# One visit of two token tiles moved from the late to the early list of a mixture layer

## The chip, the cores and the metric

The kernel runs on one core of a Trainium2 chip. The metric is the device time of one execution in microseconds. The engines are TensorE (PE), which multiplies matrices; VectorE (DVE), ScalarE (ACT) and GpSimd (POOL), which work element by element; and SyncE (SP), which issues the DMAs here. Each engine takes its instructions strictly in the order of its own program and waits on semaphores of the others.

## What is computed

Three layers in a row, all float32: attention in which each query keeps its 32 best keys; a soft mixture of 8 experts whose shares are normalised 8 times over rows and columns; and a mixture in which each token goes to its one best expert, with 288 places for each.

```python
def _moe_ref(x, w_gate, w1, w2):
    logits = x @ w_gate                       # x: 1152 x 512, 8 experts
    logits = logits - logits.max()
    P = np.exp(logits)
    for _ in range(8):
        P /= P.sum(1, keepdims=True) + 1e-09
        P /= P.sum(0, keepdims=True) + 1e-09
        P *= N / E
    for e in range(E):
        h = np.maximum(x @ w1[e], 0.0)        # 512 -> 1024
        ye = h @ w2[e]                        # 1024 -> 512
        out += P[:, e:e + 1] * ye
    return out.astype(np.float32)
```

The change concerns this middle layer. Attention before it gives x, and the third layer takes out.

## The kernel before

The 1152 tokens lie in 9 tiles of 128. A **visit** (e, a, b) computes expert e for tiles a to b-1: it goes through the 1024 hidden values in 8 blocks, and each block needs one pair of weight tiles, 128 x 512 each, of w1 (`w0h`, `w0l` in the rows, first matmuls on line 1041) and of w2 (`w1h`, `w1l`, second matmuls on line 1153). The products are float32 by parts: each operand is cut into a high part in a reduced format (`h`) and the rest (`l`), and three of the four part products are added up. A visit of two tiles has, for each block, 12 first matmuls of 256 columns and 6 second matmuls of 512, 144 in all.

Cutting a weight tile takes a load into a raw buffer (`ra`, `rb`; SyncE), a copy to the high part (ScalarE, line 975) and a subtraction for the rest. The subtraction is here called a **split**. In an early visit it is on GpSimd (line 981), in a late one on VectorE (line 978). The first matmul's result goes through ScalarE (`hh`, line 989) and VectorE (`hl`, line 991).

Early visits run beside the attention, before the shares P are known. Their sums are parked: ScalarE copies one out of PSUM (line 1142), SyncE stores it in DRAM, and later loads it again (line 1188) for VectorE to add it, times the share, to `acc` (line 1178). Late visits run when the attention is done; their sums go from PSUM to `acc` directly. Both kinds hold their first matmuls' left operands in three or four buffers, so weights can be prepared two to three blocks ahead.

Between the two lists stands the **normalisation** (`sinkhorn`, lines 1192 to 1232): 8 passes in a strict chain. In a pass VectorE runs four small instructions over rows (lines 1212 to 1215: reduce, add a constant, reciprocal, multiply), TensorE one matmul with a matrix of ones (line 1225, two records), and VectorE four over columns (lines 1218 to 1221, the same kinds).

The order of every engine's program is fixed when the kernel is built. A planner (`Order`) simulates all engines with a cost for each job and puts the jobs down as they would start; jobs with a lower rank go first among those that are ready. Visits have ranks that rise in the order of the two lists; the normalisation has the lowest, so it goes ahead of everything that is ready. The planner's costs know nothing of what engines do to each other. After the late visits of tiles 2 to 5, tiles 6 to 8 are visited, and the tokens of finished tiles are routed in between (from line 1688 on: transposes, line 1721, line 1766), and GpSimd sends their rows out with indirect DMAs (line 1781).

Of the kernel before, what the change touches and what calls it, by code (L numbers as in the profile page):

```python
# [23 lines left out]
PARTIAL = 2  # L24
WITH = 3
FILL = 390.0
EARLY = [(0, 0, 1), (1, 0, 1)] + [(e, 0, 2) for e in range(2, 8)] + [(0, 1, 4), (1, 1, 4), (2, 2, 4), (3, 2, 6), (4, 2, 6), (0, 4, 6), (1, 4, 6)]
LATE = [(5, 2, 6), (6, 2, 6), (7, 2, 6), (2, 4, 6)] + [(e, 6, 9) for e in (2, 3, 4, 5, 6, 7, 0, 1)]
ALONE = 16
FIRST = 16  # L30
ROWS = 16
# [188 lines left out]
class Net:  # L220
# [777 lines left out]
    def mixture_one(self):  # L998
        self.unit, self.chain = 0, {}
        self.left = {t: [] for t in range(self.NT)}  # L1000
        self.visits_first(PARTIAL)
        for n, v in enumerate(EARLY):
            if n < PARTIAL:
# [6 lines left out]
    def late_one(self):  # L1010
        for v in LATE[:-1]:
            self.visit(*v, whole=v[2] - v[1] == 3)
        self.visit(*LATE[-1], whole=True)
        seen = sorted((e, t) for e, a, b in EARLY + LATE for t in range(a, b))
        assert seen == [(e, t) for e in range(self.E) for t in range(self.NT)]
# [218 lines left out]
    def made_late(self, mem):  # L1234

        def more(pool, other):
            pool.free += [(self.o.t["X"], t) for _, t in other.free]
        n = LATE[-1]
        self.ff = mem.tile([128, 16, (n[2] - n[1]) * 128], F32R, name="f")
# [590 lines left out]
```

## Time and profile before

| what | before |
|---|---|
| median of 3 runs | 1176.47 us (1176.34 to 1177.87) |
| the profiled execution | 1177.07 us |
| its span, first to last instruction | 1175.2 us |
| granted TensorE clock, mean | 0.998 of full speed |
| TensorE busy | 1151.5 us (98%) |
| VectorE busy | 907.2 us (77%) |
| ScalarE busy | 729.5 us (62%) |
| GpSimd busy | 440.5 us (37%) |

A busy share over the whole span hides the stages. Up to about 565 us TensorE and VectorE are both busy nearly all the time (attention and early visits); then comes the normalisation; from 600 us on the late visits and the routing; from 1040 us the third layer. The views used are the busy time by windows, the list of waits, and the timelines of single engines, which give each instruction with its start, its length and the idle time before it.

### The profile page before, as it was taken

The page shows a single profiled execution, that of the slowest core. Times are in us where ns is not written, and L with a number is a line of the kernel's source. Part 1 is how long each engine was busy: PE and PEld are TensorE (multiplying, and loading weights), DVE is VectorE, ACT ScalarE, POOL GpSimd, SP SyncE. Part 2 cuts the span into 40 slices and gives each one's busy share as a digit, 9 for nine tenths or more (in the row PEclk, how much of TensorE's full clock was granted, in tenths as well). Part 3 has the DMA queues.
Part 4 walks back from the last instruction along what each step waited for, and adds up shares of the span by engine and source line. Part 5 has one row for each costly group of instructions (what it writes and reads, how often), then busy time and mean ns, then how long its engine had stood idle before and what let it go on. Part 6 is the DMA issues. An engine that isn't in the chain of part 4 may idle for free.

```text
span 1175.2 us, 20867 instructions
## 1 busy us (share of the span) xinstructions
PE 1151.5 (98%) x6607; PEld 1005.3 (86%) x6607; DVE 907.2 (77%) x2178; ACT 729.5 (62%) x1731; POOL 440.5 (37%) x403
## 2 busy tenths in 40 slices
PE   8999999999999999999999999999999999999997
PEld 5877888888889888888888888989999999898886
DVE  7998999999999999998655567844555555568882
ACT  7666889888788877768543334543334444258882
POOL 5466877777556744547500000100000000016541
PEclk9999999999999999999999999999999999999999
DMA  5467666655444655536555555643444444279980
GB/s 141 110 173 204 200 182 186 190 167 156 138 134 111 201 164 148 164 109 187 153 184 175 161 171 155 204 135 114 130 125 144 144 131 136 75 238 358 344 273 23
DMA packets 243607, 195.08 MB, mean 166 GB/s; under 512 B 67551, under 2 KB 186335, under 8 KB 243488
## 3 DMA queue, kind: packets, MB, share of 16 engines
q1 hardware_dynamic: 241232, 188.78, 53.8%
q0 software_dynamic: 1648, 4.73, 1.0%
q8 instruction: 54, 0.88, 0.3%
q14 instruction: 65, 0.53, 0.2%
q10 hardware_dynamic: 608, 0.15, 0.1%
HBM read 172.87 MB, written 21.33 MB: 165 GB/s over the span
## 4 chain that ended last, share of the span: by engine, by line
PE 54%; DVE 31%; ACT 6%; issue 5%; DMA 2%; POOL 1%; SPq 0%; POOLq 0%; DVEq 0%; ACTq 0%
PE yp L1041 14%; PE yp L1153 12%; PE tp L1153 8%; DVE wk L773 7%; PE tp L1041 6%; DVE m L775 6%; DVE e L784 3%; DVE hl L991 2%; DVE m L769 2%; PE yp L1372 2%; DVE wk L719 2%; DVE etl L830 2%; DVE m L721 1%; PE tp L264 1%; PE tp L1388 1%
## 5 line engine op out<-in xcount | busy, mean ns | idle before, releaser
L1781 POOL DMA_INDIRECT disp<-acc,idx x9 | 10.3, 1141 | 436.7 <-DVE run L1777 436.7
L981 POOL TENSOR_TENSOR w0l<-ra,w0h 128x512 fp32r<-128x512 f32 x104 | 134.8, 1296 | 95.0 <-ACT w0h L975 88.3
L981 POOL TENSOR_TENSOR w1l<-rb,w1h 128x512 fp32r<-128x512 f32 x104 | 134.7, 1296 | 49.8 <-ACT w1h L975 45.6
L975 ACT ACTIVATE w0h<-ra 128x512 fp32r<-128x512 f32 x211 | 131.9, 626 | 0.0
L775 DVE MAX8 m<-wk 128x8 f32<-128x576 f32 x168 | 125.0, 751 | 1.1
L975 ACT ACTIVATE w1h<-rb 128x512 fp32r<-128x512 f32 x148 | 93.3, 630 | 52.3 <-PE yp L1153 41.3
L1041 PE MATMUL yp<-xh,w0h 128*128 128x256 f32 (+2 forms) x528 | 107.2, 325 | 0.3 <-DVE hl L991 0.2
L1041 PE MATMUL yp<-xl,w0h 128*128 128x256 f32 (+2 forms) x528 | 106.7, 324 | 0.0
L1041 PE MATMUL yp<-xh,w0l 128*128 128x256 f32 (+2 forms) x528 | 106.6, 323 | 0.0
L1153 PE MATMUL yp<-w1h,hh 128*128 128x512 f32 x240 | 98.0, 408 | 0.4 <-DVE hl L991 0.4
L989 ACT ACTIVATE hh<-yp 128x256 fp32r<-128x256 f32 (+3 forms) x113 | 49.6, 439 | 76.3 <-PE yp L1041 60.0
L1041 PEld LDWEIGHTS yp<-xh,w0h 128*128 128x128 f32 x528 | 87.7, 188 | 10.1 <-DVE hl L991 1.6
L1153 PE MATMUL yp<-w1l,hh 128*128 128x512 f32 x240 | 94.2, 393 | 0.0
L1153 PE MATMUL yp<-w1h,hl 128*128 128x512 f32 x240 | 94.1, 392 | 0.0
L975 ACT ACTIVATE v<-rb 128x512 fp32r<-128x512 f32 x65 | 40.5, 629 | 79.5 <-PE yp L1153 41.8
L991 DVE SCALAR_TENSOR_TENSOR hl<-yp,hh 128x256 fp32r<-128x256 f32 (+3 forms) x113 | 55.2, 488 | 44.2 <-ACT hh L989 43.7
L1041 PEld LDWEIGHTS yp<-xh,w0l 128*128 128x128 f32 x528 | 85.1, 189 | 3.8
L1041 PEld LDWEIGHTS yp<-xl,w0h 128*128 128x128 f32 x528 | 85.0, 189 | 3.9
L1153 PE MATMUL yp<-v,f 128*128 128x512 f32 x360 | 84.4, 391 | 0.0
L773 DVE MATCH_REPLACE8 wk<-m,wk 128x576 f32<-128x576 f32 x112 | 83.2, 743 | 0.4
L1153 PEld LDWEIGHTS yp<-v,f 128*128 128x128 f32 x360 | 67.2, 188 | 13.5
L978 DVE TENSOR_TENSOR w0l<-ra,w0h 128x512 fp32r<-128x512 f32 x107 | 73.5, 687 | 0.4
(555 smaller groups left out, 3026.2 us busy)
## 6 DMA issues: line engine op xcount, KB each, us to landing
rb<-in_moe_w_dram SPq DMA_DIRECT2D x248, 256.0 KB, 3.0
ra<-in_moe_w_dram SPq DMA_DIRECT2D x245, 256.0 KB, 3.1
acc<-in_moe_w_dram SPq DMA_DIRECT2D x67, 256.0 KB, 6.0
y<-ys SPq DMA_DIRECT2D x33, 256.0 KB, 2.4
ys<-y SPq DMA_DIRECT2D x23, 256.0 KB, 3.0
vr<-in_v_dram SPq DMA_DIRECT2D x40, 128.0 KB, 2.8
disp<-z SPq DMA_DIRECT2D x6, 771.0 KB, 5.0
qg<-in_q_dram SPq DMA_DIRECT2D x63, 64.0 KB, 2.6
```

What stands on the lines that cost most here:

```text
L719: j = self.job("DVE", r, 0.73, lambda i=i: nc.vector.match_replace(wk.t, m.t[:, i], flat() if i == 0 else wk.t, LOW), deps=[j], take=[wk] ...
L769: j = j0 = self.job("DVE", r, 0.66, lambda: nc.vector.max(m.t[:, 0], flat()), deps=got, take=[m])
L773: j = self.job("DVE", r, 0.73, lambda i=i: nc.vector.match_replace(wk.t, m.t[:, i], flat() if i == 0 else wk.t, LOW), deps=[j], take=[wk] ...
L775: j = self.job("DVE", r, 0.66, lambda i=i: nc.vector.max(m.t[:, i + 1], wk.t), deps=[j], use=[wk] if i == 2 else [])
L784: masks.append(self.job("DVE", r, t_dve(288) + 0.08, lambda half=half, p=p: nc.vector.scalar_tensor_tensor(e.t[:, half * 288:(half + 1) * ...
L975: jh = self.job("ACT", -500 + rank, t_act(512, True), lambda r=r, w=w: nc.scalar.activation(w.t[0], r.t, AF.Copy), deps=[j], take=[w])
L978: jl = self.job("DVE", -100 + rank, t_dve(512, True), lambda r=r, w=w: nc.vector.tensor_sub(w.t[1], r.t, w.t[0].bitcast(F32)), deps=[jh], ...
L981: jl = self.job("POOL", -100 + rank if k > 8 * NATIVE + 4 else FIRST - 3, t_pool(512), lambda r=r, w=w: nc.gpsimd.tensor_sub(w.t[1], r.t, ...
L989: jh = self.job("ACT", -1000 + k * 0.001, t_act(b - a), lambda: nc.scalar.activation(h.t[0][:, a:b], p.t[:, :b - a], AF.Relu), deps=deps, ...
L991: jl = self.job("DVE", -1000 + k * 0.001, t_dve(b - a), lambda: nc.vector.scalar_tensor_tensor(h.t[1][:, a:b], p.t[:, :b - a], 0.0, h.t[0] ...
L1041: nc.tensor.matmul(p.t[:, :b - a], w1[0].t[i][:, d, :], self.xt[s][:, d, c0 + a:c0 + b], start=m == 0 and d == 0, stop=m == 2 and d == 3)
L1153: nc.tensor.matmul(y[t].t, h.t[i][:, c:c + 128], w2[0].t[s], start=f == 0 and m == 0, stop=f == last and m == 2)
```

## The change

The visit of expert 2, tiles 4 and 5, leaves the late list and becomes the last entry of the early list.

```diff
-EARLY = [(0, 0, 1), (1, 0, 1)] + [(e, 0, 2) for e in range(2, 8)] + [(0, 1, 4), (1, 1, 4), (2, 2, 4), (3, 2, 6), (4, 2, 6), (0, 4, 6), (1, 4, 6)]
-LATE = [(5, 2, 6), (6, 2, 6), (7, 2, 6), (2, 4, 6)] + [(e, 6, 9) for e in (2, 3, 4, 5, 6, 7, 0, 1)]
+EARLY = [(0, 0, 1), (1, 0, 1)] + [(e, 0, 2) for e in range(2, 8)] + [(0, 1, 4), (1, 1, 4), (2, 2, 4), (3, 2, 6), (4, 2, 6), (0, 4, 6), (1, 4, 6), (2, 4, 6)]
+LATE = [(5, 2, 6), (6, 2, 6), (7, 2, 6)] + [(e, 6, 9) for e in (2, 3, 4, 5, 6, 7, 0, 1)]
```

With that its 16 splits go to GpSimd, its two sums are parked and fetched back, and it stands ahead of the visit of expert 5. No instruction of TensorE is added or dropped. The two lists already end and begin in the middle of the normalisation, so the visit lands there.

GpSimd's program around the end of the early visits, before (`w0l`, `w1l` are the rests of the weight tiles; the last row is the first indirect DMA of the routing):

```order
L981 TENSOR_TENSOR w0l_80<-ra_75,w0h_79 128x512
L981 TENSOR_TENSOR w1l_90<-rb_77,w1h_89 128x512
L981 TENSOR_TENSOR w0l_82<-ra_73,w0h_81 128x512
L981 TENSOR_TENSOR w1l_92<-rb_76,w1h_91 128x512
L1781 DMA disp<-acc,idx_6557 2304x514
```

and after, from the same place on:

```order
L981 TENSOR_TENSOR w0l_82<-ra_73,w0h_81 128x512
L981 TENSOR_TENSOR w1l_92<-rb_76,w1h_91 128x512
L981 TENSOR_TENSOR w0l_84<-ra_74,w0h_83 128x512
L981 TENSOR_TENSOR w1l_86<-rb_78,w1h_85 128x512
L981 TENSOR_TENSOR w0l_80<-ra_75,w0h_79 128x512
L981 TENSOR_TENSOR w1l_88<-rb_77,w1h_87 128x512
L981 TENSOR_TENSOR w0l_82<-ra_73,w0h_81 128x512
```

Behind `w1l_92`, where the indirect DMAs of the routing followed, there are now sixteen more splits, of which five are shown.

VectorE's program at the fourth pass of the normalisation, before and after in one piece of the difference:

```order
 L1215 TENSOR_TENSOR prob<-prob,rsum 128x72
 L991 SCALAR_TENSOR_TENSOR hl_98<-yp_72,hh_97 128x256
-L978 TENSOR_TENSOR w0l_84<-ra_74,w0h_83 128x512
-L978 TENSOR_TENSOR w1l_86<-rb_78,w1h_85 128x512
 L1218 TENSOR_REDUCE csum<-tp_65 128x8
 L1219 TENSOR_SCALAR csum<-csum 128x8
 L1220 RECIPROCAL csum<-csum 128x8
 L1221 TENSOR_TENSOR prob<-prob,csum 128x72
-L991 SCALAR_TENSOR_TENSOR hl_94<-yp_71,hh_93 128x256
 L1212 TENSOR_REDUCE rsum<-prob 128x9
 L1213 TENSOR_SCALAR rsum<-rsum 128x9
```

The splits of expert 5 have left the passes; the same holds for the passes behind.

TensorE's program at the fifth and sixth pass:

```order
 L1153 MATMUL tp_67<-w1h_87,hl_98 128x512
 L1041 MATMUL tp_66<-xh,w0h_81 128x256 x4
+L1225 MATMUL tp_68<-prob,ones 128x72
 L1041 MATMUL tp_66<-xl,w0h_81 128x256 x4
 L1041 MATMUL tp_66<-xh,w0l_82 128x256 x4
-L1225 MATMUL tp_68<-prob,ones 128x72
 L1153 MATMUL yp_69<-w1h_89,hh_93 128x512
 L1153 MATMUL yp_69<-w1l_90,hh_93 128x512
```

The fifth pass's matmul stands eight matmuls earlier, and from here on there is one pass's matmul in every block of the visit, in the same place.

## Rows read from the trace of the kernel before

**Rows 1.** Windows: us, busy us (count) of PE, PEld, DVE, ACT, POOL; clock; DMA.

```profile
582.00:600.00 18.00, 17.71 (x94) 15.03 (x93) 15.76 (x55) 7.99 (x16) 0.00 (x0) 1.00 0.56 175
...
600.00:1040.00 440.00, 439.53 (x2289) 391.60 (x2288) 251.70 (x539) 176.23 (x340) 10.27 (x9) 1.00 0.47 145
```

**Rows 2.** All waits of TensorE, 560 to 1050 us: total us, times, longest.

```profile
PE tp L1225 <- DVE prob L1215: 2.2, 2, 1.9
PE yp L1202 <- DVE sk L1201: 0.5, 1, 0.5
PE tp L1398 <- DVE hl L991: 0.5, 1, 0.5
```

**Rows 3.** TensorE timeline: start us, us, instruction, [idle before <- releaser].

```profile
571.60 0.34 PE L1225 MATMUL tp<-prob,ones 128*128 128x72 f32 x2
...
576.67 0.44 PE L1225 MATMUL tp<-prob,ones 128*128 128x72 f32 x2 [1.87 <-DVE prob L1215]
...
579.81 0.34 PE L1225 MATMUL yp<-prob,ones 128*128 128x72 f32 x2
...
583.30 0.44 PE L1225 MATMUL tp<-prob,ones 128*128 128x72 f32 x2 [0.29 <-DVE prob L1215]
```

**Rows 4.** GpSimd timeline, the weight splits around the same passes.

```profile
572.23 1.28 POOL L981 TENSOR_TENSOR w1l<-rb,w1h 128x512 fp32r<-128x512 f32 x1
...
574.02 1.28 POOL L981 TENSOR_TENSOR w0l<-ra,w0h 128x512 fp32r<-128x512 f32 x1 [0.51 <-ACT w0h L975]
...
575.26 1.27 POOL L981 TENSOR_TENSOR w1l<-rb,w1h 128x512 fp32r<-128x512 f32 x1
...
579.19 1.29 POOL L981 TENSOR_TENSOR w0l<-ra,w0h 128x512 fp32r<-128x512 f32 x1 [2.66 <-ACT w0h L975]
...
580.44 1.29 POOL L981 TENSOR_TENSOR w1l<-rb,w1h 128x512 fp32r<-128x512 f32 x1
```

**Rows 5.** VectorE timeline, small instructions of the normalisation.

```profile
569.31 0.15 DVE L1207 TENSOR_SCALAR sk<-sk 128x1 f32<-128x1 f32 x1
...
572.25 1.30 DVE L1219 TENSOR_SCALAR csum<-csum 128x8 f32<-128x8 f32 x1
...
574.35 0.98 DVE L1213 TENSOR_SCALAR rsum<-rsum 128x9 f32<-128x9 f32 x1
...
575.62 1.00 DVE L1215 TENSOR_TENSOR prob<-prob,rsum 128x72 f32<-128x72 f32 x1
...
578.85 0.23 DVE L1215 TENSOR_TENSOR prob<-prob,rsum 128x72 f32<-128x72 f32 x1
...
580.45 1.30 DVE L1219 TENSOR_SCALAR csum<-csum 128x8 f32<-128x8 f32 x1
...
582.02 0.23 DVE L1221 TENSOR_TENSOR prob<-prob,csum 128x72 f32<-128x72 f32 x1
...
582.55 0.17 DVE L1213 TENSOR_SCALAR rsum<-rsum 128x9 f32<-128x9 f32 x1
...
583.01 0.23 DVE L1215 TENSOR_TENSOR prob<-prob,rsum 128x72 f32<-128x72 f32 x1
```

**Rows 6.** ScalarE timeline: weight copies, and one copy of a finished sum.

```profile
578.49 0.62 ACT L975 ACTIVATE w0h<-ra 128x512 fp32r<-128x512 f32 x1
...
581.47 0.62 ACT L975 ACTIVATE w0h<-ra 128x512 fp32r<-128x512 f32 x1
...
582.58 0.63 ACT L975 ACTIVATE w1h<-rb 128x512 fp32r<-128x512 f32 x1 [0.48 <-PE tp L1153]
...
593.19 0.59 ACT L1142 ACTIVATE yt<-yp 128x512 f32<-128x512 f32 x1
```

**Rows 7.** VectorE groups, 560 to 600 us: busy us, mean ns, idle before.

```profile
L978 DVE TENSOR_TENSOR w0l<-ra,w0h 128x512 fp32r<-128x512 f32 x5 | 3.4, 682 | 0.0
...
L978 DVE TENSOR_TENSOR w1l<-rb,w1h 128x512 fp32r<-128x512 f32 x4 | 2.7, 685 | 0.0
```

**Rows 8.** VectorE timeline, one addition of a fetched sum.

```profile
718.35 0.75 DVE L1178 SCALAR_TENSOR_TENSOR acc<-yt,prob,acc 128x512 f32<-128x512 f32 x1
```

## The prediction

> **What bounds the kernel now.** I read the windows of busy time first. From 600 to 1040 us TensorE is busy 439.53 of 440 us, while VectorE is busy 251.70 and GpSimd 10.27 [rows 1]. In that stretch, whatever delays TensorE delays the end, and relieving VectorE is worth nothing by itself. The list of TensorE's waits says the same: between 560 and 1050 us it has four stalls of note, three of them around 568 to 583 us, where the expert shares are normalised, and one of 0.5 us at the tail of the stretch [rows 2]. So the question is what the change does to TensorE just before 600 us, and whether it adds stalls after.
>
> The normalisation is eight passes. In a pass VectorE runs eight small instructions (lines 1212 to 1215 and 1218 to 1221), and TensorE one fp32 matmul, shown as two records, between the two halves (line 1225). TensorE is in order: each such matmul stands at a fixed place among the visits' matmuls, and if VectorE is late, all of TensorE waits. The places of four of them are in [rows 3]. From the first to the second are 5.07 us, with 1.87 of waiting; from the second to the third 3.14 us without any; from the third to the fourth 3.49 with 0.29. The rest have no wait [rows 2].
>
> What made the two slow passes slow is read by laying the VectorE timeline over the GpSimd one. The scalar operation of line 1219 starts at 572.25 and lasts 1.30 us; GpSimd splits a weight tile from 572.23 to 573.51 [rows 4, 5]. Line 1213 at 574.35 lasts 0.98, to 575.33; GpSimd's split ends at 575.30. Line 1215 at 575.62 lasts 1.00, to 576.62; the split of 575.26 ends at 576.53. Line 1219 at 580.45 lasts 1.30, under the split of 580.44. With GpSimd silent the same instructions take 0.17 and 0.23 us (578.85, 582.02, 582.55, 583.01) [rows 5]. So a scalar or two-tensor operation of VectorE on SBUF that starts during a GpSimd split ends only when the split does. One scalar operation did not wait: line 1207 at 569.31, one element a row, 0.15 us [rows 5].
>
> The Trainium skill has this in "SBUF — State Buffer", section "Who interferes with whom": a VectorE instruction with two SBUF inputs, or a scalar operation in a two-port mode, shares a port pair with GpSimd, and the one that issues second blocks until the first is done. This speaks against the change; the four long rows agree, the row of line 1207 shows that not every such operation is caught, and by the rule alone the sum below would be the same.
>
> In the kernel before, GpSimd's last split ends at 581.73 [rows 4], and from the fourth pass on VectorE is alone. That is what the change takes away.
>
> **The change, part by part.** Nothing moves before about 582 us: on TensorE, ScalarE, GpSimd and the DMA queue the order is the same up to there. TensorE's instructions are the same in number and shape; the 144 matmuls of the visit only stand earlier. There was no stall in the late place [rows 2] and none is left there, so I put nothing for the place it leaves.
>
> Sixteen splits go from VectorE to GpSimd. VectorE loses 16 x 0.69 = 11 us [rows 7]; behind 600 us that is worth nothing, as said. Nine of its splits stood between the passes in 583 to 600 us [rows 7]; they fall out of there (those of expert 5 come after the normalisation), but TensorE was not waiting then, so the gain is at most nothing. GpSimd gets 16 x 1.29 = 20.6 us [rows 4], from about 582 us on, beside passes four to eight. GpSimd has little else to do there: none of its time is busy from 582 to 600 us before, and 10.27 of 440 us after [rows 1].
>
> Now the passes, one by one, with the durations of the rows.
>
> Third to fourth. ScalarE's copy of the next weights ends at 581.47 + 0.62 = 582.09 [rows 6]. GpSimd starts 0.08 us behind such a copy (578.49 + 0.62 = 579.11, start 579.19) [rows 4, 6], so now at 582.17. The copy for the second split is ready at 582.58 + 0.63 = 583.21 [rows 6], and the two splits run to 583.42 and 584.71 (the second starts 1.25 us after the first and lasts 1.29, as at 580.44). VectorE gets 582.02 in ahead of it. The operation of 582.55 now waits to about 583.45, the reciprocal follows, and line 1215 at about 583.74 meets the second split and ends at 584.80. TensorE's fourth matmul moves from 583.30 to 584.85. TensorE was ready at 583.01, so the wait is 1.84 us instead of 0.29.
>
> Fourth to fifth. A wait of TensorE delays the matmuls behind it, the ScalarE copies that follow those, and so GpSimd's next pair. In the trace the pair starts 579.19 - 576.67 = 2.52 us behind such a matmul [rows 3, 4]; VectorE, left alone, needs 578.85 + 0.23 - 576.67 = 2.41 us for its eight instructions [rows 3, 5]. It is through just before the pair starts, and the fifth matmul comes at TensorE's own pace, 3.14 us on, at 587.99, without a wait.
>
> Fifth to sixth. GpSimd's pair began at 584.85 + 2.52 = 587.37, 0.62 us ahead of the fifth matmul. It was just 0.62 ahead of the third (579.19 and 579.81). The pattern repeats: 5.04 us, then 3.14, then 5.04. The eighth matmul comes at 579.81 + 3 x 5.04 + 2 x 3.14 = 601.21. At TensorE's pace it would be 579.81 + 5 x 3.14 = 595.51. The waits sum to **5.7 us** against 0.29 before, so **+5.4 us**. One disturbance: two ScalarE copies of finished sums (line 1142, 593.19, about half a microsecond apart [rows 6]) fall into the seventh pass and push GpSimd's second split about 1 us back. That changes which instruction is held in the eighth pass; worked through, it ends within 0.1 us of the same time, or, if one operation slips in ahead, 1.2 us sooner.
>
> After the eighth matmul five of the visit's eight weight pairs are still to be used. GpSimd's pair takes 581.73 - 579.19 = 2.54 us, and TensorE needs 3.14 for one with a pass's matmul in it, a little less without, so GpSimd keeps up: nothing. VectorE's first splits for expert 5 come about when GpSimd's last ends; one held split (1.3 us at most) has a whole weight pair of slack: nothing.
>
> The visit's two sums are now parked in DRAM and fetched back: two ScalarE copies at 0.59 [rows 6], two stores and two loads on SyncE's queue, between weight loads. VectorE adds from SBUF what it added from PSUM, 0.75 us each either way [rows 8]. DMA is busy 0.56 and 0.47 of the two windows [rows 1], and TensorE is fed two weight pairs ahead: nothing, and at most one stall of some 1 us if a fetch holds up a weight load. The routing of tiles 0 to 5 now falls among the visits of tiles 6 to 8; its matmuls are in order too. Before, none of its places had a wait [rows 2]: nothing, with 2 us as the bound from the longest wait of this kind, 1.87.
>
> The sum: 1177.07 (the profiled execution) + 5.4 = 1182.5. That execution lies 0.6 above the median of the runs shown, so on the median's scale 1176.47 + 5.4 = **1181.9**.
>
> **The rivals.**
> Lighter: each pass is held once and not twice, as from the third to the fourth before, 3.49 us. Then 5 x 0.35 - 0.29 = +1.5, 1177.9. For it: small shifts of ScalarE's copies can bring the passes into that step. Against it: the one place where both splits were present at the whole length of a pass (first to second) took 5.07.
> Heavier: every pass is held twice, 5 x 1.9 - 0.29 = +9.2, 1185.7. For it: GpSimd is busy 2.5 of every 3.14 us. Against it: a TensorE wait shifts GpSimd too, as after 576.67.
> The other side: the passes gain from VectorE's relief. With nine splits gone from between them, and if the splits on GpSimd hold the passes by less than TensorE's slack of 3.14 - 2.41 = 0.73 us each, no wait is left after the third pass, and the time is 1176.47 - 0.3 = 1176.2; it decides at 0.73 us. For it: line 1207 shows an operation that did not wait. Against it: the held ones lost 0.77 to 1.13 us each. The skill's "Perfetto Trace Analysis", section "Optimizing Scalar/DVE Operations", says that moving work off a saturated VectorE to GpSimd may make sense, and adds that between these two it might not help; here VectorE is not saturated where the work left.
> Later loss: the routing, in its new place, stalls TensorE once or twice on top: +7.4, 1183.9.
>
> **How the numbers follow.** Forecast 0.62 (1181.9; its own range 1180.4 to 1182.6); lighter 0.12 (1177.9); heavier 0.09 (1185.7); later loss 0.05 (1183.9); the other side 0.12, of which 0.08 within 0.2% and 0.04 faster, should VectorE's relief be worth something that these rows don't show. A measurement of this kernel can tell about 0.2%, 2.35 us, from no change, so 1178.8 is the border: slower 0.62 + 0.09 + 0.05 = 0.76, same 0.12 + 0.08 = 0.20, faster 0.04. The range takes in lighter and heavier and leaves out the other side: 1177.8 to 1185.8.
>
> **What would show it.** In the profile after: waits of TensorE on line 1215 of 1.8 to 1.9 us, at the fourth, sixth and eighth matmuls of line 1225, some 7.5 us in all instead of 2.2; rows of lines 1213, 1215, 1219 of 0.8 to 1.3 us, each under a GpSimd split, after 582 us; the eighth matmul near 601; no wait behind it up to the last visit. It is wrong if those rows are short though GpSimd splits beside them, if the waits fall on every pass or are a third of that, or if TensorE waits between 610 and 1000 us.

## The result, and the profile after

The changed kernel is slower: 1186.11 us (median of 4 runs, 1185.21 to 1187.10) against 1176.64 (median of 4, 1176.34 to 1177.87), a ratio of 1.0069 with a 95% interval of 1.0054 to 1.0083 (the two medians by themselves give 1.0080). The forecast was 1181.9, in a range from 1177.8 to 1185.8. The direction came as said; the loss of 9.5 us between the medians is 4 us above the 5.4 forecast, and the median lies 0.3 us over the top of the range; by the ratio the time is 1176.47 x 1.0069 = 1184.6, inside it. The profiled execution, the fastest of the four, took 1185.21, with a span of 1183.4 us, 8.2 above that of before. These 8.2 us are the part that a trace can account for.

All waits of TensorE from 560 to 1060 us after the change (releaser, us in total, times, longest), the answer to [rows 2]:

```profile
PE tp L1225 <- DVE prob L1215: 5.5, 3, 1.9
PE yp L1225 <- DVE prob L1215: 0.6, 1, 0.6
PE yp L1202 <- DVE sk L1201: 0.5, 1, 0.5
PE tp L1398 <- DVE hl L991: 0.5, 1, 0.5
```

The waits on the passes' matmul are 6.1 us in four places instead of 2.2 in two; nothing else is new. TensorE's timeline (start, duration, instruction, idle before and releaser) gives the places, as in [rows 3]; the last row is the first 512-column matmul of expert 5's visit, the next one in the program:

```profile
576.68 0.44 PE L1225 MATMUL tp<-prob,ones 128*128 128x72 f32 x2 [1.87 <-DVE prob L1215]
...
579.82 0.34 PE L1225 MATMUL yp<-prob,ones 128*128 128x72 f32 x2
...
584.83 0.44 PE L1225 MATMUL tp<-prob,ones 128*128 128x72 f32 x2 [1.81 <-DVE prob L1215]
...
589.53 0.34 PE L1225 MATMUL tp<-prob,ones 128*128 128x72 f32 x2
...
593.32 0.44 PE L1225 MATMUL yp<-prob,ones 128*128 128x72 f32 x2 [0.59 <-DVE prob L1215]
...
596.46 0.34 PE L1225 MATMUL tp<-prob,ones 128*128 128x72 f32 x2
...
601.46 0.44 PE L1225 MATMUL tp<-prob,ones 128*128 128x72 f32 x2 [1.81 <-DVE prob L1215]
...
619.75 1.07 PE L1041 MATMUL yp<-xh,w0h 128*128 128x512 f32 x4
```

The fourth, sixth and eighth pass wait, the fifth and seventh do not, as said. VectorE's timeline, with the GpSimd timeline behind it, shows by what; they answer to [rows 5] and [rows 4]:

```profile
582.57 0.93 DVE L1213 TENSOR_SCALAR rsum<-rsum 128x9 f32<-128x9 f32 x1
...
583.77 1.00 DVE L1215 TENSOR_TENSOR prob<-prob,rsum 128x72 f32<-128x72 f32 x1
...
585.58 0.17 DVE L1219 TENSOR_SCALAR csum<-csum 128x8 f32<-128x8 f32 x1
...
589.90 0.23 DVE L1218 TENSOR_REDUCE csum<-tp 128x8 f32<-128x72 f32 x1 [2.33 <-PE tp L1225]
...
592.24 1.02 DVE L1215 TENSOR_TENSOR prob<-prob,rsum 128x72 f32<-128x72 f32 x1
```

```profile
582.18 1.28 POOL L981 TENSOR_TENSOR w0l<-ra,w0h 128x512 fp32r<-128x512 f32 x1 [0.45 <-ACT w0h L975]
583.42 1.27 POOL L981 TENSOR_TENSOR w1l<-rb,w1h 128x512 fp32r<-128x512 f32 x1
...
591.89 1.28 POOL L981 TENSOR_TENSOR w0l<-ra,w0h 128x512 fp32r<-128x512 f32 x1 [0.93 <-ACT w0h L975]
```

The row of 582.57 ends at 583.50 and GpSimd's split at 583.46; 583.77 ends at 584.77 and the split at 584.69; 592.24 ends at 593.26 and the split at 593.17. The row of 585.58, with GpSimd silent, takes 0.17. (That of 589.90 is used further below.)

What the forecast did not have is in TensorE's windows of one microsecond (window, length, busy us and instructions, granted clock, DMA share, GB/s):

```profile
585.00:586.00 1.00, 1.00 (x10) 1.00 0.81 213
586.00:587.00 1.00, 1.00 (x5) 0.51 0.73 213
587.00:588.00 1.00, 1.00 (x4) 0.50 0.06 21
588.00:589.00 1.00, 1.00 (x5) 0.50 0.00 0
589.00:590.00 1.00, 1.00 (x9) 0.78 0.15 41
...
603.00:604.00 1.00, 1.00 (x4) 0.55 0.45 168
604.00:605.00 1.00, 1.00 (x4) 0.50 0.00 0
605.00:606.00 1.00, 1.00 (x6) 0.50 0.00 0
606.00:607.00 1.00, 1.00 (x9) 0.75 0.48 137
```

Behind the waits of the fourth and the eighth pass TensorE's clock was granted at 0.50 of full speed, which is 1.2 instead of 2.4 GHz, for a little over 3 us each; TensorE is busy all the while and does half as many matmuls. What was lost is the sum of 1 minus the clock over these windows: 1.71 us and 1.70 us, 3.4 together.

Behind the normalisation nothing more is lost. The last wait of the list, at the end of the last visit, stands at 1040.04 us, where it stood at 1032.50 before:

```profile
1040.04 0.40 PE L1398 MATMUL tp<-hl,w1h 128*128 128x288 f32 x1 [0.46 <-DVE hl L991]
```

That is 7.54 us later; the other 0.7 of the span's 8.2 come at the very end, behind the last step of the chain that ended last (1167.17 us, 1159.64 before, 7.53 apart), and were only read.

### The profile page after: what moved, and what is told of

The parts are those of the page before. It is cut to its first block, busy times and chain, and to the rows that moved or that the text cites. A ratio compares the mean times of both kernels' runs of the same rounds, so it can differ in the third digit from the quotient of the medians.

```text
span 1183.4 us, 20874 instructions
## 1 busy us (share of the span) xinstructions
PE 1155.1 (98%) x6607; PEld 1007.6 (85%) x6607; DVE 904.4 (76%) x2162; ACT 731.4 (62%) x1733; POOL 460.6 (39%) x419
## 4 chain that ended last, share of the span: by engine, by line
PE 56%; DVE 31%; ACT 6%; issue 4%; POOL 1%; DMA 1%; SPq 0%; POOLq 0%; DVEq 0%; ACTq 0%
PE yp L1153 13%; PE tp L1041 12%; PE yp L1041 9%; PE tp L1153 7%; DVE wk L773 7%; DVE m L775 6%; DVE e L784 3%; PE yp L1372 2%; DVE hl L991 2%; DVE m L769 2%; DVE wk L719 2%; PE tp L264 1%; DVE etl L830 1%; DVE m L721 1%; PE tp L1388 1%
## 5 line engine op out<-in xcount | busy, mean ns | idle before, releaser
L981 POOL TENSOR_TENSOR w0l<-ra,w0h 128x512 fp32r<-128x512 f32 x112 | 145.1, 1295 | 104.7 <-ACT w0h L975 99.0
L1041 PE MATMUL tp<-xl,w0h 128*128 128x512 f32 (+2 forms) x364 | 83.2, 350 | 0.0
L1041 PE MATMUL tp<-xh,w0h 128*128 128x512 f32 (+2 forms) x364 | 82.8, 350 | 0.0
L1041 PE MATMUL yp<-xh,w0h 128*128 128x256 f32 (+2 forms) x436 | 82.4, 311 | 0.3 <-DVE hl L991 0.3
L1041 PE MATMUL tp<-xh,w0l 128*128 128x512 f32 (+2 forms) x364 | 82.3, 348 | 0.0
L1041 PE MATMUL yp<-xl,w0h 128*128 128x256 f32 (+2 forms) x436 | 82.0, 310 | 0.0
L1041 PE MATMUL yp<-xh,w0l 128*128 128x256 f32 (+2 forms) x436 | 81.8, 309 | 0.0
L991 DVE SCALAR_TENSOR_TENSOR hl<-tp,hh 128x512 fp32r<-128x512 f32 (+2 forms) x74 | 41.8, 565 | 48.7 <-ACT hh L989 48.6
L989 ACT ACTIVATE hh<-tp 128x512 fp32r<-128x512 f32 (+2 forms) x74 | 37.0, 500 | 63.9 <-PE tp L1041 59.9
L1041 PEld LDWEIGHTS yp<-xh,w0h 128*128 128x128 f32 x436 | 70.4, 188 | 6.6 <-DVE hl L991 1.6
```

Of the source, the lines that this page charges most:

```text
L981: jl = self.job("POOL", -100 + rank if k > 8 * NATIVE + 4 else FIRST - 3, t_pool(512), lambda r=r, w=w: nc.gpsimd.tensor_sub(w.t[1], r.t, ...
L989: jh = self.job("ACT", -1000 + k * 0.001, t_act(b - a), lambda: nc.scalar.activation(h.t[0][:, a:b], p.t[:, :b - a], AF.Relu), deps=deps, ...
L991: jl = self.job("DVE", -1000 + k * 0.001, t_dve(b - a), lambda: nc.vector.scalar_tensor_tensor(h.t[1][:, a:b], p.t[:, :b - a], 0.0, h.t[0] ...
L1041: nc.tensor.matmul(p.t[:, :b - a], w1[0].t[i][:, d, :], self.xt[s][:, d, c0 + a:c0 + b], start=m == 0 and d == 0, stop=m == 2 and d == 3)
```

## The experiments

The kernels are compared by ratio to the kernel before, run on the same chip beside them. It had medians of 1177.44 us (31 runs, beside e1, e2, e3 and e5) and 1177.42 us (22 runs, beside the others). The ratios and their intervals decide; they are not quite those of the medians (for e3, 1184.85 to 1177.44 would be 1.0063).

| kernel | median us | ratio | 95% interval |
|---|---|---|---|
| e1, after, moved visit split on VectorE | 1178.70 | 1.0009 | 0.9995 to 1.0022 |
| e2, before, visit first in the late list | 1181.30 | 1.0030 | 1.0019 to 1.0042 |
| e3, after, waits filled with idle matmuls | 1184.85 | 1.0051 | 1.0035 to 1.0067 |
| e5, before, last early splits on VectorE | 1174.51 | 0.9973 | 0.9961 to 0.9985 |
| e4, before, ten idle GpSimd subtractions | 1188.45 | 1.0092 | 1.0075 to 1.0109 |
| e6, before, ten idle GpSimd fills | 1179.02 | 1.0011 | 1.0000 to 1.0022 |
| e7, after, as e5 and e1 together | 1174.85 | 0.9971 | 0.9959 to 0.9983 |
| after, once more | 1186.47 | 1.0074 | 1.0060 to 1.0089 |

**e1: the moved visit, split on VectorE.** The visit stands in the early list as in the changed kernel, its sums are parked, the routing moves; only its 16 splits stay on VectorE.

```diff
-            w1, w2 = self.weights(..., f, late=not early, ...
+            w1, w2 = self.weights(..., f, late=not early or (e, t0) == (2, 4), ...
```

> The changed kernel, but the 16 splits of the moved visit stay on VectorE; its place, its parked sums and the fetches stay as changed. Theory (GpSimd's splits hold VectorE's small instructions of the normalisation, TensorE waits, and after two of these waits its clock is granted at half for some 3 us): after 582 us no row of lines 1213, 1215, 1219, 1221 above 0.3 us, waits of TensorE on line 1225 of at most 0.6 us in all behind the third pass, clock 1.00 from 570 to 620 us, time 1176 to 1177.5. Rival (the loss comes from the place of the visit, the parked sums or the routing in its new place): time stays at 1183 to 1187.

Measured: 1.0009, no difference that the interval shows. TensorE's timeline of e1 at the passes; its first wait, of 1.87 us on the second pass, is that of the kernel before:

```profile
579.53 0.34 PE L1225 MATMUL yp<-prob,ones 128*128 128x72 f32 x2
583.02 0.44 PE L1225 MATMUL tp<-prob,ones 128*128 128x72 f32 x2 [0.29 <-DVE prob L1215]
...
611.93 1.07 PE L1041 MATMUL yp<-xh,w0h 128*128 128x512 f32 x4
...
1032.21 0.40 PE L1398 MATMUL tp<-hl,w1h 128*128 128x288 f32 x1 [0.46 <-DVE hl L991]
```

The waits on the passes are those of before, 1.87 and 0.29, and the clock stays at 1.00 from 582 to 616 us. From the third pass's matmul to the first matmul of expert 5 are 611.93 - 579.53 = 32.40 us; in the changed kernel 619.75 - 579.82 = 39.93, with the same instructions on TensorE in between. The difference, 7.53, is the whole lag of the changed kernel up to 1167 us. From there to the last wait of the list it is 420.28 us in e1 and 420.29 in the changed kernel, and from the third pass to that wait 452.68 in e1 and 452.69 before. So the loss goes with the splits' engine, and place, parking and routing together make none that can be measured. One thing besides the engine differs: the planner, which knows where the splits are, puts the matmuls of passes four to eight 3.50 to 4.09 us apart in e1, where two of them without a wait are 3.14 apart in the changed kernel. A test in which nothing moves on TensorE is e4.

**e2: the same visit in another place, without GpSimd.** The kernel before, with the visit at the head of the late list.

```diff
-LATE = [(5, 2, 6), (6, 2, 6), (7, 2, 6), (2, 4, 6)] + ...
+LATE = [(2, 4, 6), (5, 2, 6), (6, 2, 6), (7, 2, 6)] + ...
```

> The kernel before, with the visit at the head of the late list: TensorE works on it at the same place as in the changed kernel, but splits are on VectorE and no sum is parked. Theory: 1176 to 1177.5, within 0.5 us of the changed kernel with its splits on VectorE; the difference of the two is what parking and fetching cost. Rival (place and routing): 1183 to 1187 again. If parking were the cause, this one is at 1176 and the one with the splits on VectorE near 1185.

Measured: 1.0030; the expectation missed. The waits on the passes are those of before (2.2 us in two places), no small VectorE instruction is held behind the third pass, and the clock stays full from 570 to 620 us, but the visit of expert 5, which now follows, has two waits in its first blocks, on VectorE's addition to `acc` and on `hl`:

```profile
624.88 1.20 PE L1041 MATMUL yp<-xh,w0h 128*128 128x512 f32 x4 [1.44 <-DVE acc L1178]
...
629.30 1.19 PE L1041 MATMUL yp<-xh,w0h 128*128 128x512 f32 x4 [1.41 <-DVE hl L991]
```

They are 2.85 us, and a ratio of 1.0030 is 3.5. As read, the sums of a late visit keep their PSUM buffers until VectorE has added them, while those of an early one are copied away; this was not tried. It is a cost of that place in the late list, and e1 shows that the changed kernel does not have it.

**e3: the waits filled.** The changed kernel with six idle matmuls (bf16, 512 columns, into the pass's own bank) ahead of the matmul of the fourth, sixth and eighth pass, so that TensorE works while it would wait.

```diff
+                if turn in (3, 5, 7):
+                    w = self.ones_b
+                    for _ in range(6):
+                        nc.tensor.matmul(b.t, w, w[:, None, :].to_broadcast([128, 4, 128]), start=True, stop=True)
                 nc.tensor.matmul(b.t[:, :NT * E], self.ones, flat, start=True, stop=True)
```

> The changed kernel with six idle matmuls of 512 columns, some 1.35 us, ahead of the normalisation matmul of passes 4, 6 and 8, where TensorE waits. Theory on the clock (it is granted at half because TensorE stood idle): no half clock between 582 and 610 us, the waits shrink to about 0.5 us each, and the visit's lag goes from 7.5 to about 5.5 us: 1183 to 1184. Rival (the clock falls for another cause, for example the load of that stretch): the half clock stays and the time is 1185 to 1187, or more where the idle matmuls are not covered.

Measured: 1.0051; the median, 1184.85, lies 0.85 us over the 1183 to 1184 expected, and the profiled execution was the slowest of its runs, 1187.11 us. Its line for the window from 582 to 600 us (busy us and count of PE, PEld, DVE, ACT, POOL; clock; DMA share; GB/s), and that of the changed kernel:

```profile
582.00:600.00 18.00, 16.99 (x103) 13.68 (x102) 14.94 (x41) 8.09 (x17) 11.39 (x10) 1.00 0.54 157
```

```profile
582.00:600.00 18.00, 15.26 (x87) 13.24 (x85) 13.63 (x39) 7.83 (x16) 11.37 (x9) 0.91 0.54 163
```

The clock is 1.00 instead of 0.91, with GpSimd as busy. TensorE's timeline of e3, in which the pass's matmul is line 1231 and the fill line 1230 (the seventh pass's, at 597.15, is left out):

```profile
580.83 0.34 PE L1231 MATMUL yp<-prob,ones 128*128 128x72 f32 x2
...
583.87 1.47 PE L1230 MATMUL tp<-ones_b 128*128 128x512 bf16 x6
...
585.85 0.44 PE L1231 MATMUL tp<-prob,ones 128*128 128x72 f32 x2 [0.51 <-DVE prob L1215]
...
588.99 0.34 PE L1231 MATMUL tp<-prob,ones 128*128 128x72 f32 x2
...
594.00 0.44 PE L1231 MATMUL yp<-prob,ones 128*128 128x72 f32 x2 [0.51 <-DVE prob L1215]
...
602.16 0.44 PE L1231 MATMUL tp<-prob,ones 128*128 128x72 f32 x2 [0.51 <-DVE prob L1215]
```

The periods from the third matmul on are 5.02, 3.14, 5.01, 3.15 and 5.01 us. That is the pattern of the forecast, 5.04 and 3.14. Each of the three fills is over 0.51 us before VectorE lets the pass's matmul go, so they delay nothing. From the third pass to the first matmul of expert 5 it takes 38.09 us (580.83 to 618.92), 5.69 more than e1 and 1.84 less than the changed kernel. So the held passes alone cost 5.7, and the half clock 1.84 on top, net of the waiting that it takes away. The whole gain from after to e3 is not that well known: the two ratios' intervals overlap, and in e3's profiled execution the clock was also at half in two other places, at 98 and at 1030 us. That the waits bring the half clock rests on this one profile with fills, against three without (the changed kernel twice, and e4 below) that have it behind the fourth pass.

**e5: the same cause in the kernel before.** In that kernel too a visit of the early list, (1, 4, 6), has its last splits beside the first passes [rows 4]. They are moved to VectorE, for the blocks from the sixth on.

```diff
-            w1, w2 = self.weights(..., f, late=not early, ...
+            w1, w2 = self.weights(..., f, late=not early or (e, t0) == (1, 4) and f > 4, ...
```

> The kernel before, with the splits of the last three blocks of its last early visit (expert 1, tiles 4 and 5) on VectorE instead of GpSimd. Theory: the rows of 0.98 to 1.30 us in the first three passes shrink to 0.17 to 0.23, the waits of 1.87 and 0.29 us go, and the time falls by 1 to 2.2 us, to 1174.3 to 1175.5. Rival (VectorE's own splits take the place of the holds in the passes): the waits stay or change place and the time is 1176 to 1178.

Measured: 0.9973, 2.9 us less than the kernel before by the medians. No wait on line 1225 is left, and the operation of line 1219 that took 1.30 in the first pass [rows 5] takes 0.17:

```profile
571.34 0.17 DVE L1219 TENSOR_SCALAR csum<-csum 128x8 f32<-128x8 f32 x1
```

The two waits were 2.2 us in the profile, within the interval of the gain (1.8 to 4.6 us). This version beats both kernels.

**e4: GpSimd's work without the visit.** The kernel before with ten idle subtractions of 128 x 512 on GpSimd, back to back, behind its last split (two clears of their inputs, 1.03 us together, are VectorE's).

```diff
+            if turn > 2:
+                for _ in range(2):
+                    self.job("POOL", 0, 1.29, lambda: nc.gpsimd.tensor_sub(self.dum[0], self.dum[1], self.dum[2]), deps=[j])
```

> The kernel before, nothing moved; GpSimd runs ten idle subtractions of the size of a split (two inputs and the output in SBUF) back to back behind its last split, from about 582 us on, and nothing uses their result. VectorE clears two buffers ahead of the normalisation for them, about 1 us in all. Theory (an occupied GpSimd holds VectorE's scalar and two-tensor operations): rows of lines 1213, 1215, 1219, 1221 and of VectorE's own splits last 0.7 to 1.9 us from 582 to 595 us, TensorE waits on line 1225, and the time is 1181 to 1186 (on the scale of a kernel before at 1176.6). Rival (place, parking or the planner's order is the cause): 1176.5 to 1178.

Measured: 1.0092, though no visit moved and nothing needs what GpSimd makes. The median, 1188.45, is 2.5 us over the range expected; the profiled execution, 1185.11, was the fastest of four and has a span 8.1 us longer than before. The rows of GpSimd and of VectorE, and TensorE's waits from 560 to 1060 us:

```profile
581.61 14.61 POOL L1229 TENSOR_TENSOR dum<-dum,dum 128x512 f32<-128x512 f32 x10
```

```profile
593.34 1.12 DVE L1215 TENSOR_TENSOR prob<-prob,rsum 128x72 f32<-128x72 f32 x1
...
596.94 0.17 DVE L1219 TENSOR_SCALAR csum<-csum 128x8 f32<-128x8 f32 x1
```

```profile
PE tp L1225 <- DVE prob L1215: 7.6, 3, 3.0
PE yp L1202 <- DVE sk L1201: 1.5, 1, 1.5
PE yp L1225 <- DVE prob L1215: 0.6, 1, 0.6
```

The passes are held as long as GpSimd works, to 596.22 us, and not after. The new waits are 6.0 us on line 1225 and 1.0 on line 1202 (the clears), and the clock was at half from 586 to 590 us, 1.7 us more by its windows. From the third pass's matmul (579.74) to the last wait of the list (1040.64) are 460.90 us, 8.2 more than before, of which these waits on line 1225 and the clock make 7.8. (The 1.0 of the clears comes before that; it does not show in the span because this profile lacks the half clock at 19 to 23 us, 1.7 us by its windows, that the one of before has.) Here VectorE's own splits stand between the passes too, and of the four beside GpSimd's work three took 1.56, 1.77 and 1.78 us, and one (594.38) its usual 0.68 [rows 7]. GpSimd lost as well: most of its subtractions took 1.28 us, but the longest 1.77, and the ten 14.61, where ten at the pace of the splits in [rows 4], 1.25 us apart, would take some 12.5 by estimate.

**e6: the same, but GpSimd only writes.** Ten fills in place of the ten subtractions.

```diff
-                    self.job("POOL", 0, 1.29, lambda: nc.gpsimd.tensor_sub(self.dum[0], self.dum[1], self.dum[2]), deps=[j])
+                    self.job("POOL", 0, 1.29, lambda: nc.gpsimd.memset(self.dum[0], 0.0), deps=[j])
```

> The same, but the ten idle GpSimd instructions only write (they fill the buffer with zeros) and read no SBUF. It tells the kinds of VectorE instruction apart and is the control for the two clears. Theory that it takes a GpSimd instruction that reads to hold a two-tensor operation: rows of lines 1215 and 1221 stay at 0.23 us, rows of 1213 and 1219 may be held for the length of one filling; time within 1.5 us of the kernel before. Theory that any GpSimd instruction holds both: rows of all four lines are lengthened.

Measured: 1.0011. The fills are shorter and are over by 587.68 us, so they lie beside the end of the third pass, the fourth, and the first half of the fifth:

```profile
581.90 5.78 POOL L1229 MEMSET dum<- 128x512 f32 x10
```

```profile
580.69 1.76 DVE L1219 TENSOR_SCALAR csum<-csum 128x8 f32<-128x8 f32 x1
...
582.73 0.23 DVE L1221 TENSOR_TENSOR prob<-prob,csum 128x72 f32<-128x72 f32 x1
...
583.26 0.36 DVE L1213 TENSOR_SCALAR rsum<-rsum 128x9 f32<-128x9 f32 x1
...
583.90 0.23 DVE L1215 TENSOR_TENSOR prob<-prob,rsum 128x72 f32<-128x72 f32 x1
...
585.85 0.17 DVE L1219 TENSOR_SCALAR csum<-csum 128x8 f32<-128x8 f32 x1
...
587.03 0.17 DVE L1213 TENSOR_SCALAR rsum<-rsum 128x9 f32<-128x9 f32 x1
```

The multiplications of two tensors (582.73, 583.90) lie under the fills and take 0.23, as with GpSimd silent; under a GpSimd operation that reads they took about 1.0. Of the scalar operations two are held: 0.36 instead of 0.17 (583.26, under the fill of 583.07, which ends at 583.59), and 1.76 for the one that met GpSimd's last split, which ended at 581.97, and the first fill. Two are not (585.85, 587.03); each started less than 0.1 us before the end of a fill (585.40 and 586.57, 0.53 us each), so these rows can't tell a short hold from none. In "SBUF — State Buffer", section "Who interferes with whom", the Trainium skill says that a VectorE instruction with two SBUF inputs contends with a GpSimd instruction that reads SBUF and not with one that only writes it, while scalar operations in a two-port mode contend with GpSimd whichever it does. The two-tensor rows agree, and so do the two long scalar rows; that the scalar operations here run in such a mode is not shown by any row.

**e7: both together.** The changed kernel with the splits of both visits on VectorE.

```diff
+... late=not early or (e, t0) == (2, 4) or (e, t0) == (1, 4) and f > 4, ...
```

> The changed kernel with the splits of the moved visit and of the last three blocks of the visit before it (expert 1, tiles 4 and 5) on VectorE, so that GpSimd is silent beside all eight passes. Theory: no wait on line 1225 and the time of the kernel before with those three blocks on VectorE, 0.25 to 0.3% under the kernel before; the early place itself is worth nothing. Rival (the early place is worth something once the holds are gone): 0.4% or more under the kernel before.

Measured: 0.9971, no wait on line 1225 and the clock at 1.00 from 582 to 616 us. That is e5's 0.9973: with the splits out of the way, the early place of the visit gives or takes nothing that can be measured (each ratio is known to 0.0012).

**The changed kernel once more.**

> The changed kernel as it is, beside the others on one chip: 1.0055 to 1.0085 of the kernel before by either theory; the profile has waits of 1.8 us at passes 4 and 8 and half the clock behind one or both of them.

Measured: 1.0074, as at first. The waits come again (1.81, 0.59, 1.81 us); the half clock came again from 586 to 590 us, but not behind the eighth pass, and in another place, at 1030 us, where e3's profiled execution had it as well:

```profile
604.00:606.00 2.00, 2.00 (x16) 1.00 0.00 0
...
1032.00:1034.00 2.00, 2.00 (x11) 0.50 0.00 0
```

At 1030 us no wait precedes it: TensorE has none between the eighth pass and 1041 us, and was busy, just before, mostly with matmuls of 96 and 8 columns. The changed kernel's first profile has the clock at 1.00 there (1030 to 1035 us).

So the waits are the kernel's, and how much clock is lost behind them, and where else, differs between executions.

## Why the prediction was right, and where its size was off

**The cause held.** GpSimd's splits hold VectorE's scalar and two-tensor instructions, TensorE waits in order: e1 takes the splits off GpSimd and the loss is gone; e4 adds GpSimd's work to a kernel in which nothing moved (and two clears, 1.0 us) and has a loss of the same size; and the held rows end within 0.1 us of the split beside them. The fourth matmul was put at 584.85 with 1.84 of waiting, and came at 584.83 with 1.81; e3, which keeps the clock up, has the forecast's periods to 0.03 us throughout. The sum of 5.4 for the held passes answers to 5.69 there. (The 583.42 given as the end of the fourth pass's first split is the start of the second; the first ended at 583.46, and the sum does not hang on it.)

**The zeros held.** Place, parking and routing were put at nothing. By its time alone e1 leaves room for up to 2.6 us (1.0022), and e7 against e5 (0.9971, 0.9973) for about 2; by the profiles e1 and the kernel before are within 0.01 us of each other from the third pass to 1032 us. VectorE's relief, which e1 and e7 do not have, was put at nothing too: behind the passes the changed kernel, which has it, takes the same 420.3 us as e1.

**The step that failed is the one behind a wait of TensorE.** "A wait of TensorE delays the matmuls behind it" was priced as the wait alone, and "the pattern repeats" followed from it. But behind two of the three waits the clock was at half. From the fourth to the fifth matmul are 4.70 us instead of 3.14. That changed what GpSimd met. VectorE waited 2.33 us for the fifth matmul and went on at 589.90, when the first split of the pair (587.38 to 588.66) was over and had held nothing; two operations of that pass were held instead of three, and the wait at the sixth was 0.59 instead of 1.90. The eighth came at 601.46, near the 601.21 forecast, because one error gave back most of the other: 1.56 lost before the fifth matmul, 1.25 won before the sixth (3.79 instead of 5.04). That the eighth matmul is where it was forecast is in this part luck. Then the second stretch of half clock followed, unforecast. The account up to expert 5 is: waits 1.81 + 0.59 + 1.81 = 4.2 us instead of 5.7 (so the list of waits shows 6.1 in all, where some 7.5 were forecast), less the 0.29 of before, plus 3.4 for the clock, 7.3; measured were 7.53. With the 0.7 at the end of the kernel that is the span's 8.2.

**What stays open.** The first wait, 1.87 us at 576.67, has no half clock behind it, before or after, and the second, of 1.81 us and 8.2 us later, has. In e4 a wait of 2.79 has it and the next one, of 2.98, has not; and at 1030 us it came without a wait. So why the clock fell behind these waits could not be read from these runs: that filling them keeps it up is what e3 shows, in one profile. Nor is it settled why the medians lie 9.5 apart and the spans 8.2; the stretches of half clock that come in other places in some executions (19 to 23 us in the profiles before and after, 1021 us in e7's, 1030 us in two others) are of a size for that, but no run ties them to it.

**The rivals.** Lighter (held once a pass) falls: the rows show both splits holding in the fourth pass. Heavier has a time near the result (1185.7), but not its mechanism: the fifth and seventh passes have no wait. The other side falls, since the held instructions of the fourth pass lost about 0.8 us each (0.93 instead of 0.17, 1.00 instead of 0.23), together 1.5, where it needed less than 0.73 in a pass. Later loss falls: no wait between 610 and 1040 us is new.

## What to carry to other kernels

Before work is moved to an idle GpSimd, lay it over VectorE's timeline: if it reads SBUF beside a strict chain of small VectorE instructions on which an in-order TensorE waits, each scalar or two-tensor one of them can be held to the end of the GpSimd instruction, here 1 us where 0.2 would do. Price a stall of TensorE as more than its length, since the clock may be at half behind it. And when a rule explains a loss, look for the same pattern in the kernel before: here that gave the version that is faster than both.

## What the runs showed of the hardware

- Waits of TensorE of 1.8 us were in places followed by a stretch at half clock (0.50 from 587 to 589 us) that cost 1.7 us, about as much as the wait; with idle matmuls in the waits the clock stayed at 1.00 there, in the one execution that was profiled. Half clock also came with no wait ahead of it, at 1021 us in e7's profile and at 1030 us in two others.
- Contention goes both ways: of ten GpSimd subtractions that met VectorE's instructions the longest took 1.77 us, against 1.29 alone, and three of VectorE's splits beside them 1.56 to 1.78, against 0.69.
- What GpSimd does matters: under fills, which only write, two-tensor multiplications of VectorE took 0.23 us, and under subtractions about 1.0.
- Not every small instruction of VectorE is held: in the kernel before, a reduction (574.09) and a reciprocal (575.37) that started during a GpSimd split took 0.23 and 0.21 us, as they do with GpSimd silent.
